# Local/global attention with an MLP: casts of w_out on VectorE, half of batch 1's planes on GpSimd and VectorE, output groups in one piece, global values 64 columns wide

## The chip, the cores and the metric

The kernel runs on one core of one Trainium2 chip. Its time is the device time of one execution in microseconds (us). Of the kernel before, three runs are known, 959.68, 959.82 and 957.89 us, with a median of 959.68. Beside them one execution was taken with the hardware profiler.

## The reference

There are 8 batches of 8 heads with a head size of 64. Each has 512 local tokens and 32 global ones; q, k and v are given apart for both. After the attention every token goes through an MLP with w_in (512 x 2048) and w_out (2048 x 512). Cut to what matters:

```python
def sm(s):
    s = s - np.max(s, axis=-1, keepdims=True)
    e = np.exp(s)
    return e / (np.sum(e, axis=-1, keepdims=True) + 1e-09)

out_g = sm(scale * q_g @ k_all.T) @ v_all           # a global token sees all 544 keys
s_ll = np.where(abs(i - j) <= 32, scale * q_l @ k_l.T, -1e9)
s_lg = scale * q_l @ k_g.T                          # a local one sees the 32 global keys
out_l = sm(concat([s_lg, s_ll])) @ v_all            # and a band of 65 local ones
x = concat([out_g, out_l]).reshape(8 * 544, 512)
h = x @ w_in
return (h * np.cos(h)) @ w_out
```

## The kernel before, in words

**Two planes for each number.** Every matrix that the tensor engine (PE) multiplies is split into a high and a low plane of 16-bit floats, hi = cast(z) and lo = cast(z - hi). A product takes three matmuls: hi by hi, hi by lo and lo by hi. The engines beside PE are ScalarE (ACT), VectorE (DVE) and GpSimd (POOL); all DMAs are issued by SyncE (SP).

**The weights.** They arrive as 64-bit floats. `decode` (L227 to L232) makes 32-bit floats from such a piece: ACT reads the high words (L227), DVE shifts the low words (L228) and joins them (L232). `split_w` (L238) then casts the high plane on ACT (L239) and subtracts it on POOL in two halves (`pool_tt`, L213). Before that, each piece's maximum is taken by DVE (L246), for which pieces 8 to 15 of w_out are loaded once more (`raw_wm`, L388). `w_out_piece` (L397 on) decodes the sixteen pieces of 128 rows of w_out, two in each of the slots 1 to 8, that is, while the first chunks of the MLP already run.

**The attention.** It goes by pairs of heads, four pairs in a batch. `load_qk` brings q and k of a pair (L441, three buffers), `load_v` v of a batch. `v_a` finds the maximum of v: for batches 0 and 1 by four ACT instructions (L476) and a small reduction, from batch 2 on by one DVE reduction (L481); QMA sets which batches take which. `sc_a` multiplies q and k (L527) for four tiles of 128 queries, each against a window of 192 or 224 keys; the exponentials (L425) are on ACT. `sc_d` (L567 on) scales them by the reciprocal sum and writes both planes. It has several forms, chosen by a table. Form 1, which all of batch 1 takes, is two ACT instructions for the high planes (L592) and two DVE ones for the low planes (L593). Form 3 multiplies on POOL (L578), casts on ACT (L584) and subtracts on POOL (L586). Then the planes are transposed by DMA, and `av_a` (L624 on) multiplies them by v (L645). The global queries have their own steps: `g_f` (L728 on) multiplies the transposed weights `ptg` by v into `gacc` (L737), `g_g` scales the result into `xg` (L750).

**The MLP.** Tokens go through in chunks of 256, sixteen of local tokens and one of the globals, with eight slots to a chunk; a slot is 256 of the 2048 hidden columns. In a slot, `m1_a` is 24 matmuls into `ph` (L801, three PSUM buffers). ACT, DVE, ACT, POOL, DVE, ACT and POOL then make h cos(h) in planes `gh` and `gl` (L823 to L846). Three slots later `m2_a` (L849 on) is twelve matmuls of 512 columns into `po_0` and `po_1` (L860 hi by w_out's hi, L861 hi by its lo, L862 lo by its hi). `po` has two buffers, so chunk 1's `m2_a` can't begin before chunk 0's is finished and read out.

**The order of the work.** Each step has a slot and a priority, given by calls `at(slot, priority, function, ...)` (L941 on). A scheduler then puts every instruction in a fixed order on its engine, by these priorities and by when it reckons the inputs to be there. Batch 0's attention lies ahead of slot 0, batch 1's in the slots of chunks 0 and 1, beside the pieces of w_out; later batches run spread out, one ahead of their chunks.

Of the kernel before, what the change touches and what calls it, by code (L numbers as in the profile page):

```python
# [10 lines left out]
F32 = mybir.dt.float32  # L11
# [4 lines left out]
ALU = mybir.AluOpType  # L16
# [3 lines left out]
P = 128  # L20
# [3 lines left out]
SG = 32  # L24
D = 64
# [3 lines left out]
NJ = DF // P  # L29
# [29 lines left out]
PL0 = 0  # L59
PL1 = 1  # L60
VE = [1, 4, 4]
# [6 lines left out]
TPV = [1, 0, 1, 0]  # L68
WLV = 0
DI = 3  # L70
QMA = 2
KQB = 3
# [46 lines left out]
def body(tc, qf, v, wi, wo, mask, out):  # L119
# [5 lines left out]
    with ExitStack() as ctx:  # L125
# [111 lines left out]

        def split_w(h, l, z, on_vector=False):  # L238
            nc.scalar.copy(h, z)  # L239
            if on_vector:  # L240
                nc.vector.tensor_tensor(l, z, h, op=ALU.subtract)
            else:
                pool_tt(l, z, h, ALU.subtract)
# [153 lines left out]
        def w_out_piece(j):  # L397
# [6 lines left out]
            decode(z, raw, wsc, low_after="wsc")  # L404
            split_w(wo_h[:, j], wo_l[:, j], z, j % 4 < WLV)

# [108 lines left out]
        def sc_a(b, p, i):  # L515
# [7 lines left out]
            for j, c in ((i, slice(0, w0)), (i + 1, slice(w0, w0 + w1_))):  # L523
                z, w = WIN[j]
                for h in range(2):
                    r = slice(D * h, D * h + D)
                    nc.tensor.matmul(  # L527
                        pt[h][:, c], q[r, QZ[j] : QZ[j] + P], k[r, z : z + w], start=True, stop=True,
                        skip_group_check=True,
                    )  # L530
# [36 lines left out]
        def sc_d(b, p, i):  # L567
# [3 lines left out]
            w = WIN[i][1]  # L571
            pl = PLS[p][i] if b == 0 else (PL0, PL1, PL)[min(b, 2)]
            if pl in (3, 4):
                if pl == 3:
                    r = rr[:, 2 * i : 2 * i + 2]
# [7 lines left out]
                lo = planes[i][:, :, 1, OFF[i] : OFF[i] + w]  # L583
                nc.scalar.copy(hi, t)  # L584
                for h in range(2):
# [38 lines left out]
        def av_a(b, p):  # L624
# [5 lines left out]
            )  # L630
            for k, (tl, segs) in enumerate(plan):
                for ip, (vt, pl) in enumerate(((vh, 0), (vh, 1), (vl, 0))):
# [95 lines left out]
        def g_f(b, g):  # L728
            ptg = st.pop(("ptg", b, g))
            acc = ps.tile([P, 2, SG], F32, tag="att", name=f"gacc_{b}_{g}")  # L730
            for a in range(2):
                vh, vl = st["v", b, 2 * g + a]
                for tl in range(NT):
                    for ip, (vt, pl) in enumerate(((vh, 0), (vh, 1), (vl, 0))):
                        for h in range(2):
                            hh = 2 * a + h
                            mm = nc.tensor.matmul(  # L737
                                acc[64 * h : 64 * h + 64, a],
                                vt[:, tl, 64 * h : 64 * h + 64],
                                ptg[:, pl * NT + tl, 32 * hh : 32 * hh + 32],  # L740
                                start=(a == 0 and tl == 0 and ip == 0),
                                stop=(a == 1 and tl == NT - 1 and ip == 2),
                                skip_group_check=True,
# [5 lines left out]
        def g_g(b, g):  # L749
            nc.vector.tensor_scalar(  # L750
                xg[:, 2 * g : 2 * g + 2, b * SG : (b + 1) * SG], st.pop(("gacc", b, g)),
                pvs[:, b : b + 1], None, op0=ALU.mult,
            )

# [94 lines left out]
        def m2_a(c, j):  # L849
            gh, gl = st.pop(("g2", c, j))  # L850
            if j == 0:
                st["po", c] = [
                    ps.tile([P, DM], F32, tag="po", name=f"po_{c}_{k}", bufs=2) for k in range(CT // P)
                ]
            po = st["po", c]
            for k in range(CT // P):
                for a in range(2):
                    q = slice(a * CT + k * P, a * CT + (k + 1) * P)
                    f = 2 * j + a
                    nc.tensor.matmul(po[k], gh[:, q], wo_h[:, f], start=(f == 0), stop=False)  # L860
                    nc.tensor.matmul(po[k], gh[:, q], wo_l[:, f], start=False, stop=False)  # L861
                    nc.tensor.matmul(po[k], gl[:, q], wo_h[:, f], start=False, stop=(f == NJ - 1))  # L862

# [221 lines left out]
```

## Time and profile before

| what | before |
|---|---|
| median of three runs | 959.68 us (957.89 to 959.82) |
| the profiled execution | 959.23 us |
| its span (first to last instruction) | 957.5 us |
| mean granted clock of PE | 0.965 |
| PE busy | 909.4 us (95%) |
| ACT busy | 668.4 us (70%) |
| DVE busy | 569.3 us (59%) |
| POOL busy | 399.7 us (42%) |

A busy share is that of the whole span; it hides that the first fifth of the span is not like the rest. The page's second part shows this in 40 equal slices: PE is at nine tenths or more from the seventh slice on, and mostly lower before. Which engine sets the pace is read for each stage from a view that cuts the span at given times. A row of the timeline has a start, a length, the engine, the line and the operation, with what ended the idle time ahead of it in brackets. Matmuls overlap, and their ends are modelled, so the pace of PE is the difference of two starts.

### The profile page before, as it was taken

How to read it: one execution, taken by the hardware profiler on the slowest of the kernel's cores; microseconds unless marked ns; L12 is line 12 of the kernel's file. 1: busy time of each engine (PE TensorE's matmuls, PEld its weight loads, DVE VectorE, ACT ScalarE, POOL GpSimd, SP SyncE). 2: the span in 40 equal slices, each digit the busy share in tenths (PEclk: the TensorE clock that was granted, in tenths of full speed). 3: DMA queues.
4: the chain of work that ended last, by engine and by line, in shares of the span. 5: the costliest groups of instructions: out<-in, count | busy, mean ns of one | idle time of the engine just before them, and what ended most of it. 6: DMA issues, size and time to landing. Idle time of an engine off the chain costs nothing.

```text
span 957.5 us, 20487 instructions
## 1 busy us (share of the span) xinstructions
PE 909.4 (95%) x7963; PEld 604.0 (63%) x7963; DVE 569.3 (59%) x1544; ACT 668.4 (70%) x1435; POOL 399.7 (42%) x412
## 2 busy tenths in 40 slices
PE   6657989999999999999999999999999999999995
PEld 4446656656666666666666666666666666766663
DVE  5987978746565656566655656564746554423231
ACT  7886899957787677766777778777777775443341
POOL 5856654443334243434343333324343434444441
PEclk8667989999999999999999999999999999999998
DMA  9936167745232533545262725342443333000000
GB/s 371 386 121 198 34 163 162 152 111 125 49 108 43 157 63 71 108 122 111 56 122 50 183 46 129 46 146 46 119 61 71 81 68 58 23 1 23 1 24 22
DMA packets 155178, 96.44 MB, mean 101 GB/s; under 512 B 141000, under 2 KB 141128, under 8 KB 153288
## 3 DMA queue, kind: packets, MB, share of 16 engines
q1 hardware_dynamic: 155080, 95.13, 39.6%
q8 instruction: 62, 1.02, 0.4%
q14 instruction: 36, 0.29, 0.1%
HBM read 51.59 MB, written 8.91 MB: 63 GB/s over the span
## 4 chain that ended last, share of the span: by engine, by line
PE 51%; ACT 15%; DVE 11%; issue 9%; POOL 8%; DMA 5%; SPq 0%; ACTq 0%; POOLq 0%; DVEq 0%
PE ph L801 21%; PE po L861 8%; PE po L862 8%; PE po L860 8%; ACT t L425 4%; DMA vr<-v 3%; POOL w L839 3%; PE ps L527 3%; POOL gl L846 2%; ACT planes L592 2%; PE acc L645 2%; DVE gf L841 2%; ACT gh L845 2%; ACT L425 2%; POOL wi_l L213 2%
## 5 line engine op out<-in xcount | busy, mean ns | idle before, releaser
L801 PE MATMUL ph<-xh,wi_h 128*128 128x256 f16 x1024 | 280.7, 274 | 0.9 <-DVE gf L841 0.5
L801 PE MATMUL ph<-xl,wi_h 128*128 128x256 f16 x1024 | 279.8, 273 | 0.0
L801 PE MATMUL ph<-xh,wi_l 128*128 128x256 f16 x1024 | 279.8, 273 | 0.0
L846 POOL TENSOR_TENSOR gl<-gf,gh 128x512 f16<-128x512 f32 x136 | 163.4, 1202 | 237.1 <-ACT gh L845 237.0
L839 POOL TENSOR_TENSOR w<-w 128x512 f32<-128x512 f32 x136 | 143.6, 1056 | 259.1 <-ACT w L425 241.2
L801 PEld LDWEIGHTS <-wi_h 128*128 128x128 f16 x2176 | 205.9, 98 | 55.4 <-issue 18.8
L861 PE MATMUL po<-wo_hl,gh 128*128 128x512 f16 x544 | 206.7, 380 | 0.6 <-POOL wo_hl L213 0.6
L860 PE MATMUL po<-wo_hl,gh 128*128 128x512 f16 x544 | 204.7, 380 | 1.7 <-ACT wo_hl L239 1.7
L862 PE MATMUL po<-wo_hl,gl 128*128 128x512 f16 x544 | 206.3, 380 | 0.0
L845 ACT CAST gh<-gf 128x512 f16<-128x512 f32 x136 | 83.4, 615 | 112.8 <-DVE gf L841 112.7
L824 DVE SCALAR_TENSOR_TENSOR u<-u,cm,ph 128x512 f32<-128x512 f32 x136 | 101.1, 744 | 101.0 <-ACT u L823 101.0
L841 DVE SCALAR_TENSOR_TENSOR gf<-w,ph 128x512 f32<-128x512 f32 x136 | 93.1, 684 | 110.6 <-POOL w L839 110.1
L425 ACT ACTIVATE w<-u,ca 128x512 f32<-128x512 f32 x136 | 98.1, 722 | 84.4 <-DVE u L824 83.5
L425 ACT ACTIVATE t<-t,mn 128x192 f32<-128x192 f32 (+1 forms) x256 | 117.3, 463 | 18.5 <-DVE mn L545 18.1
L801 PEld LDWEIGHTS <-wi_l 128*128 128x128 f16 x1088 | 106.7, 98 | 13.4 <-issue 0.5
L823 ACT ACTIVATE u<-ph,cm 128x512 f32<-128x512 f32 x136 | 92.3, 679 | 25.2 <-PE ph L801 25.2
L593 DVE SCALAR_TENSOR_TENSOR planes<-t,sm,planes 128x192 f16<-128x192 f32 (+1 forms) x232 | 97.8, 481 | 12.0 <-ACT planes L592 11.2
L545 DVE CUSTOM_DVE_ANT_0 t<-ps,msk 128x192 f32<-128x192 f32 (+1 forms) x256 | 83.2, 367 | 18.0 <-PE ps L527 14.8
L862 PEld LDWEIGHTS <-gl 128*128 128x128 f16 x544 | 53.3, 98 | 63.1 <-issue 0.9
L592 ACT ACTIVATE planes<-t,sm 128x192 f16<-128x192 f32 (+1 forms) x232 | 86.3, 458 | 0.0
L861 PEld LDWEIGHTS <-gh 128*128 128x128 f16 x544 | 53.3, 98 | 51.5 <-issue 2.5
L860 PEld LDWEIGHTS <-gh 128*128 128x128 f16 x544 | 52.8, 98 | 51.4 <-issue 2.6
(149 smaller groups left out, 1098.5 us busy)
## 6 DMA issues: line engine op xcount, KB each, us to landing
qkr<-qf SPq DMA_DIRECT2D x31, 608.0 KB, 5.0
vr<-v SPq DMA_DIRECT2D x8, 1280.0 KB, 6.5
out<-o SPq DMA_DIRECT2D x34, 256.0 KB, 2.0
raw_wi<-wi SPq DMA_DIRECT2D x6, 1024.0 KB, 12.2
wo_hl<-wo SPq DMA_DIRECT2D x8, 512.0 KB, 12.7
raw_wm<-wo SPq DMA_DIRECT2D x8, 512.0 KB, 5.7
raw_wo<-wo SPq DMA_DIRECT2D x8, 512.0 KB, 4.4
raw_wi<-wi SPq DMA_DIRECT2D x4, 512.0 KB, 12.3
```

The costliest lines, as they stand in the source:

```text
L425: ins = nc.scalar.activation(*a, **k).ins
L592: a = nc.scalar.activation(hi, t[:, h], AF.Identity, scale=r)
L593: d = nc.vector.scalar_tensor_tensor(lo, t[:, h], r, hi, op0=ALU.mult, op1=ALU.subtract)
L801: nc.tensor.matmul(ph[:, a], w[:, kc, f], x[:, kc, q], start=first and ip == 0, stop=last and ip == 2, skip_group_check=True,)
L824: nc.vector.scalar_tensor_tensor(u, u, m, ph, op0=ALU.subtract, op1=ALU.subtract)
L839: nc.gpsimd.tensor_tensor(w, w, w, op=ALU.mult)
L841: nc.vector.scalar_tensor_tensor(gf, w, 0.5, st.pop(("ph", c, j)).rearrange("p a b -> p (a b)"), op0=ALU.subtract, op1=ALU.mult,)
L845: nc.scalar.copy(gh, gf)
L846: nc.gpsimd.tensor_tensor(gl, gf, gh, op=ALU.subtract)
L860: nc.tensor.matmul(po[k], gh[:, q], wo_h[:, f], start=(f == 0), stop=False)
L861: nc.tensor.matmul(po[k], gh[:, q], wo_l[:, f], start=False, stop=False)
L862: nc.tensor.matmul(po[k], gl[:, q], wo_h[:, f], start=False, stop=(f == NJ - 1))
```

## The change

It has five parts.

- All sixteen high planes of w_out are cast by DVE (L239 before, L243 after) in place of ACT.
- Batch 1's tiles 0 and 2 of each pair take a new form 5 of `sc_d`: POOL multiplies, DVE casts both halves at once, POOL subtracts. Tiles 1 and 3 stay in form 1.
- In chunks 0 and 1 the six products of a slot for one `po` buffer are taken in another order (`MR`, `terms`), which begins with a product that needs the later of the slot's two pieces of w_out.
- `g_f` multiplies v's high plane by both planes of the weights in one matmul of 64 columns; `gacc` gets a further dimension of two, which `g_g` adds with a second DVE instruction.
- Batch 1's maximum of v goes to DVE (QMA), and its scores and its values by v are done in reversed order (SR, AR).

```diff
-PL1 = 1
+PL1 = [5, 1, 5, 1]
+MR = 2
+SR = (1,)
+AR = (1,)
+WH = "DDDDDDDDDDDDDDDD"
-QMA = 2
+QMA = 1
...
-        def split_w(h, l, z, on_vector=False):
-            nc.scalar.copy(h, z)
+        def split_w(h, l, z, on_vector=False, cast="A"):
+            {"A": nc.scalar.copy, "D": nc.vector.tensor_copy, "G": nc.gpsimd.tensor_copy}[cast](h, z)
...
-            split_w(wo_h[:, j], wo_l[:, j], z, j % 4 < WLV)
+            split_w(wo_h[:, j], wo_l[:, j], z, j % 4 < WLV, WH[j])
...
-                for h in range(2):
+                for h in (1, 0) if b in SR else (0, 1):
...
-            pl = PLS[p][i] if b == 0 else (PL0, PL1, PL)[min(b, 2)]
-            if pl in (3, 4):
-                if pl == 3:
+            pl = PLS[p][i] if b == 0 else PL1[i] if b == 1 else PL
+            if pl in (3, 4, 5):
+                if pl in (3, 5):
...
-                nc.scalar.copy(hi, t)
+                (nc.vector.tensor_copy if pl == 5 else nc.scalar.copy)(hi, t)
...
-            for k, (tl, segs) in enumerate(plan):
+            for k, (tl, segs) in enumerate(plan[::-1] if b in AR else plan):
...
-            acc = ps.tile([P, 2, SG], F32, tag="att", name=f"gacc_{b}_{g}")
+            acc = ps.tile([P, 2, 2, SG], F32, tag="att", name=f"gacc_{b}_{g}")
...
-                    for ip, (vt, pl) in enumerate(((vh, 0), (vh, 1), (vl, 0))):
+                    for ip, (vt, n) in enumerate(((vh, 2), (vl, 1))):
...
-                                acc[64 * h : 64 * h + 64, a],
+                                acc[64 * h : 64 * h + 64, a, :n],
-                                ptg[:, pl * NT + tl, 32 * hh : 32 * hh + 32],
+                                ptg[:, tl : tl + NT * (n - 1) + 1 : NT, 32 * hh : 32 * hh + 32],
...
+            nc.vector.tensor_scalar(x, acc[:, :, 1], pv, None, op0=ALU.mult)
+            nc.vector.scalar_tensor_tensor(x, acc[:, :, 0], pv, x, op0=ALU.mult, op1=ALU.add)
...
+            terms = [(a, g, w) for a in range(2) for g, w in ((gh, wo_h), (gh, wo_l), (gl, wo_h))]
+            if c < MR:
+                terms = [terms[i] for i in (4, 5, 2, 1, 3, 0)]
             for k in range(CT // P):
...
+                for i, (a, g, w) in enumerate(terms):
+                    nc.tensor.matmul(
+                        po[k], g[:, a * CT + k * P : a * CT + (k + 1) * P], w[:, 2 * j + a],
+                        start=(j == 0 and i == 0), stop=(j == NS - 1 and i == 5),
+                    )
```

The scheduler orders anew, so the change moves more than it edits. Three places are shown. Line numbers of the new kernel are four to six higher than those of the same lines before, and the number at the end of a name differs between the kernels.

The first is the end of w_out's decoding. On ACT before, from the last piece's first step to its cast (`z_wo_1854`; `wo_hl` holds both planes of w_out); `planes_76` to `planes_82` are the four tiles of a pair, `t` the exponentials:

```order
L227 ACTIVATE z_wo_1854<-raw_wo_1852,wsc 128x512
L592 ACTIVATE planes_76<-t_3_0_2200,sm_3_2376 128x192 x2
L592 ACTIVATE planes_78<-t_3_1_2204,sm_3_2376 128x224 x2
L592 ACTIVATE planes_80<-t_3_2_2214,sm_3_2376 128x224 x2
L592 ACTIVATE planes_82<-t_3_3_2218,sm_3_2376 128x192 x2
L511 ACTIVATE vh_2_3050<-vr_1717,vs_1863 128x640
L823 ACTIVATE u_5_2420<-ph_5_2395,cm_1249 128x512
L845 CAST gh_2_2107<-gf_2_2110 128x512
L714 ACTIVATE planes_g<-gt_1_2079,gsm_1_2385 128x544
L665 ACTIVATE xh_1993<-acc_2_2436,xs 128x512
L239 CAST wo_hl<-z_wo_1854 128x512
```

On ACT after, at the same place; the last piece is `z_wo_1813` here, its cast on DVE:

```order
L429 ACT_TABLE_LOAD
L429 ACTIVATE w_4_2243<-u_4_2242,ca_1201 128x512
L849 CAST gh_1_1983<-gf_1_1986 128x512
L596 ACTIVATE planes_78<-t_3_1_2165,sm_3_2320 128x224 x2
L231 ACTIVATE z_wo_1813<-raw_wo_1811,wsc 128x512
L596 ACTIVATE planes_82<-t_3_3_2179,sm_3_2320 128x192 x2
L718 ACTIVATE planes_g<-gt_1_2040,gsm_1_2329 128x544
L849 CAST gh_2_2068<-gf_2_2071 128x512
L515 ACTIVATE vh_1_2602<-vr_1674,vs_1822 128x640
L515 ACTIVATE vh_2_2977<-vr_1674,vs_1822 128x640
```

The cast of w_out is gone from ACT, and so are the writes of tiles 0 and 2 (`planes_76`, `planes_80`). On DVE before, from the low words of the last piece on:

```order
L228 TENSOR_SCALAR raw_wo_1852<-raw_wo_1852 128x512
L564 TENSOR_SCALAR sm_3_2376<-sm_3_2376 128x8
L565 RECIPROCAL sm_3_2376<-sm_3_2376 128x8
L750 TENSOR_SCALAR xg<-gacc_0_2314,pvs 128x2x32
L709 TENSOR_SCALAR gsm_1_2385<-gsm_1_2385 128x1
L710 RECIPROCAL gsm_1_2385<-gsm_1_2385 128x1
L512 SCALAR_TENSOR_TENSOR vl_1_2657<-vr_1717,vs_1863,vh_1_2656 128x640
L232 SCALAR_TENSOR_TENSOR z_wo_1854<-z_wo_1854,raw_wo_1852 128x512
L593 SCALAR_TENSOR_TENSOR planes_76<-t_3_0_2200,sm_3_2376,planes_76 128x192
L841 SCALAR_TENSOR_TENSOR gf_4_2391<-w_4_2280,ph_4_2254 128x512
L593 SCALAR_TENSOR_TENSOR planes_76<-t_3_0_2200,sm_3_2376,planes_76 128x192
```

On DVE after:

```order
L243 CAST wo_hl<-z_wo_1804 128x512
L569 RECIPROCAL sm_3_2320<-sm_3_2320 128x8
L714 RECIPROCAL gsm_1_2329<-gsm_1_2329 128x1
L232 TENSOR_SCALAR raw_wo_1811<-raw_wo_1811 128x512
L549 ISA t_0_0_2269,mn_0_0_2270<-ps_0_0_1_2259,msk 128x192
L549 ISA mn_0_0_2270 128x1
L549 ISA t_0_1_2273,mn_0_1_2274<-ps_0_0_1_2259,msk 128x224
L549 ISA mn_0_1_2274 128x1
L597 SCALAR_TENSOR_TENSOR planes_78<-t_3_1_2165,sm_3_2320,planes_78 128x224 x2
L236 SCALAR_TENSOR_TENSOR z_wo_1813<-z_wo_1813,raw_wo_1811 128x512
L597 SCALAR_TENSOR_TENSOR planes_82<-t_3_3_2179,sm_3_2320,planes_82 128x192 x2
L243 CAST wo_hl<-z_wo_1813 128x512
```

The cast of a piece (L243) stands behind its join (L236), and the last one ahead of the cast of tile 0 (L588, `planes_76`, which is the next row but one).

The second place is SP's queue about the loads for the maxima of w_out; `qkr_1` is q and k of pair 1. Before:

```order
L388 DMA raw_wm_1008<-wo 128x512
L388 DMA raw_wm_1011<-wo 128x512
L388 DMA raw_wm_1014<-wo 128x512
L441 DMA qkr_1_1413<-qf 128x1216
L388 DMA raw_wm_1017<-wo 128x512
L441 DMA qkr_2_1576<-qf 128x1216
```

After:

```order
L392 DMA raw_wm_1008<-wo 128x512
L392 DMA raw_wm_1011<-wo 128x512
L392 DMA raw_wm_1014<-wo 128x512
L392 DMA raw_wm_1017<-wo 128x512
L445 DMA qkr_1_1369<-qf 128x1216
L406 DMA raw_wo_1515<-wo 128x512
L445 DMA qkr_2_1533<-qf 128x1216
```

The load of the last maximum (`raw_wm_1017`) stands ahead of the load of pair 1, and one load of a piece (`raw_wo_1515`) ahead of that of pair 2.

The third place is PE at the end of chunk 0's output. Before, the last matmuls into `po_0` and `po_1`, which take w_out's last piece; `acc_3` is a pair's values, and the last matmul of chunk 1's `ph_7` stands 35 rows above the first row:

```order
L861 LDWEIGHTS gh_7_1786
L861 MATMUL po_0_1382<-wo_hl,gh_7_1786 128x512
L862 LDWEIGHTS gl_7_1787
L862 MATMUL po_0_1382<-wo_hl,gl_7_1787 128x512
L861 LDWEIGHTS gh_7_1786
L861 MATMUL po_1_1383<-wo_hl,gh_7_1786 128x512
L862 LDWEIGHTS gl_7_1787
L862 MATMUL po_1_1383<-wo_hl,gl_7_1787 128x512
```

After, the end of the last group of twelve (it begins 18 rows above) and what follows:

```order
L865 LDWEIGHTS gh_7_1745
L865 MATMUL po_1_1338<-wo_hl,gh_7_1745 128x512
L865 LDWEIGHTS gh_7_1745
L865 MATMUL po_1_1338<-wo_hl,gh_7_1745 128x512
L865 LDWEIGHTS gh_7_1745
L865 MATMUL po_1_1338<-wo_hl,gh_7_1745 128x512
L805 LDWEIGHTS wi_h
L805 MATMUL ph_7_2522<-xh_1038,wi_h 128x256
```

The eight products of the slot that stood apart ahead of these four are now in one piece with them, and chunk 1's `ph_7` (24 matmuls) comes behind the group.

More of the change, by code (lines that the diff above doesn't have):

```diff
@@ L737, in g_f @@
                             mm = nc.tensor.matmul(
-                                acc[64 * h : 64 * h + 64, a],
+                                acc[64 * h : 64 * h + 64, a, :n],
                                 vt[:, tl, 64 * h : 64 * h + 64],
-                                ptg[:, pl * NT + tl, 32 * hh : 32 * hh + 32],
+                                ptg[:, tl : tl + NT * (n - 1) + 1 : NT, 32 * hh : 32 * hh + 32],
                                 start=(a == 0 and tl == 0 and ip == 0),
-                                stop=(a == 1 and tl == NT - 1 and ip == 2),
+                                stop=(a == 1 and tl == NT - 1 and ip == 1),
                                 skip_group_check=True,
@@ L749, in g_g @@
         def g_g(b, g):
[L750 to L753, printed above, removed]
+            acc, pv = st.pop(("gacc", b, g)), pvs[:, b : b + 1]
+            x = xg[:, 2 * g : 2 * g + 2, b * SG : (b + 1) * SG]
+            nc.vector.tensor_scalar(x, acc[:, :, 1], pv, None, op0=ALU.mult)
+            nc.vector.scalar_tensor_tensor(x, acc[:, :, 0], pv, x, op0=ALU.mult, op1=ALU.add)
         mp = None
@@ L855, in m2_a @@
             po = st["po", c]
+            terms = [(a, g, w) for a in range(2) for g, w in ((gh, wo_h), (gh, wo_l), (gl, wo_h))]
+            if c < MR:
+                terms = [terms[i] for i in (4, 5, 2, 1, 3, 0)]
             for k in range(CT // P):
[L857 to L862, printed above, removed]
+                for i, (a, g, w) in enumerate(terms):
[3 more added lines that the diff above has]
+                    )
         def m2_b(c, k):
```

## The prediction

> **What bounds the kernel now.** I read the busy share in 40 slices first: the tensor engine (PE) is at 9 from the seventh slice (144 us) on and mostly below that ahead of it. So the view of stretches came next, for the two stages that end where PE becomes full, and for one of the full part. The columns are the stretch, its length, then busy time and instructions of PE, PE's weight loads, VectorE (DVE), ScalarE (ACT) and GpSimd (POOL), the granted clock, the DMA share and the rate:
>
> ```profile
> 92.00:128.00 36.00, 34.45 (x289) 22.36 (x288) 34.19 (x77) 31.28 (x61) 24.23 (x26) 0.96 0.20 65
> 128.00:186.00 58.00, 53.36 (x477) 33.78 (x475) 48.39 (x151) 57.79 (x134) 26.09 (x30) 0.94 0.75 164
> 306.00:408.40 102.40, 102.29 (x939) 67.91 (x938) 62.73 (x175) 75.08 (x167) 38.05 (x34) 1.00 0.45 96
> ```
>
> In the full part PE is busy 102.29 of 102.40 us: there only fewer or shorter PE instructions shorten the run, and DVE and ACT have over a quarter free. Between 128 and 186 us ACT works 57.79 of 58.00: this stage is ACT's. Between 92 and 128 DVE is the fullest but for PE (34.19 of 36.00). PE is idle for 1.55 + 4.64 = 6.2 us in both, which bounds what they can give, beside a clock of 0.94 to 0.96 there.
>
> Then the waits of the second stage and the chain that ended last, to see what ACT holds up (waits: total, times, longest; chain: start, length, engine, line):
>
> ```profile
> POOL wo_hl L213 <- ACT wo_hl L239: 15.1, 7, 4.7
> ```
>
> ```profile
> 177.65 2.60 ACT planes L592 x7
> ...
> 183.65 0.52 ACT wo_hl L239
> ...
> 186.15 0.38 PE po L861
> 186.53 0.22 PE po L862
> ```
>
> The last piece of w_out is decoded by DVE, waits for ACT behind seven plane writes, is cast by ACT, subtracted by POOL, and at 186.15 PE takes it. From there on PE is full: call 186.15 the gate. It opens the chunk's PSUM buffers for chunk 1. A move of the gate is a gain only less the PE work that is left behind it.
>
> **Global values, 64 columns at once.** PE's timeline of one group, and of the local values, which already have 64 columns (start, length; lengths overlap, so differences of starts count):
>
> ```profile
> 367.18 0.22 PE L737 MATMUL gacc<-ptg,vh 128*64 128x32 f16 x4
> 367.24 0.19 PE L737 MATMUL gacc<-ptg,vl 128*64 128x32 f16 x2
> ...
> 379.85 0.23 PE L645 MATMUL acc<-pt,vh 128*64 128x64 f16 x4
> 379.91 0.20 PE L645 MATMUL acc<-pt,vl 128*64 128x64 f16 x2
> ```
>
> A round is two vl matmuls and four vh; the four took 0.06 us (367.18 to 367.24). Four matmuls of 64 columns took 0.06 too (379.85 to 379.91), so 64 columns cost what 32 do; two of them instead of four save 0.03 a round and 0.30 us a group, which has ten rounds (two pairs of heads by five tiles of keys). The groups that lie behind the gate are counted by the next row, of the lines from 186 us on:
>
> ```profile
> L750 DVE TENSOR_SCALAR xg<-gacc,pvs 128x64 f32<-128x64 f32 x13 | 3.6, 278 | 0.0
> ```
>
> Thirteen groups in the part where PE is full: 13 x 0.30 = **-3.9 us**. The other bound is that 64 columns cost twice 32, which saves 0; I take the first, since its row is the same shape on the same engine. The read-out becomes two DVE instructions, 0.28 us more for each group. It is hidden under PE in the full part (DVE 62.73 of 102.40); without that cover it would be 16 x 0.28 = 4.5 us.
>
> **The start.** The last maximum of w_out waits for its load, which SyncE issues behind one of q and k, and the maximum of batch 1's v (L481) now lies on DVE near 47 us, where ACT did it. DVE's timeline, SyncE's, and the group of L481:
>
> ```profile
> 49.73 0.39 DVE L545 CUSTOM_DVE_ANT_0 t<-ps,msk 128x224 f32<-128x224 f32 x1 [1.76 <-POOL planes L586]
> 54.10 0.36 DVE L545 CUSTOM_DVE_ANT_0 t<-ps,msk 128x192 f32<-128x192 f32 x1 [0.44 <-POOL planes L586]
> 83.83 0.69 DVE L246 TENSOR_REDUCE wos<-raw_wm 128x1 f32<-128x512 f32 x1 [1.51 <-DMA raw_wm<-wo]
> 87.99 0.69 DVE L246 TENSOR_REDUCE wos<-raw_wm 128x1 f32<-128x512 f32 x1 [3.47 <-DMA raw_wm<-wo]
> ```
>
> ```profile
> 80.25 0.33 SPq L388 DMA_DIRECT2D raw_wm<-wo  x1
> 82.63 0.33 SPq L441 DMA_DIRECT2D qkr<-qf  x1
> 83.06 0.37 SPq L388 DMA_DIRECT2D raw_wm<-wo  x1
> ```
>
> ```profile
> L481 DVE TENSOR_REDUCE vm<-vr 128x1 f32<-128x2560 f32 x6 | 16.9, 2820 | 14.8 <-DMA vr<-v 14.8
> ```
>
> The load without one of q and k ahead of it was used 3.6 us after its issue (80.25 to 83.83), the one behind it 4.9 us (83.06 to 87.99). In the new order it takes the place of 82.63 and is used near 86.2: 1.8 us earlier. The qkr load goes back by one issue, 0.4 us, and its two other buffers hide that; were they not full ahead of need, 0.4 us comes back. L481 costs 2.82 us, of which 1.76 + 0.44 = 2.2 fills idle time: +0.6. Scales and first piece: **1.2 us earlier** (0 if another chain holds the start, 1.8 if L481 is hidden whole).
>
> **From ACT to DVE and POOL.** The rows: the cast and lo planes that go, then the nearest of those that come.
>
> ```profile
> L239 ACT CAST wo_hl<-z_wo 128x512 f16<-128x512 f32 x16 | 9.7, 614 | 2.6 <-DVE z_wo L232 2.6
> ```
>
> ```profile
> L593 DVE SCALAR_TENSOR_TENSOR planes<-t,sm,planes 128x192 f16<-128x192 f32 (+1 forms) x32 | 12.9, 449 | 0.6 <-ACT planes L592 0.6
> L592 ACT ACTIVATE planes<-t,sm 128x192 f16<-128x192 f32 (+1 forms) x32 | 11.9, 457 | 0.0
> ```
>
> ```profile
> L720 DVE CAST planes_g<-gt 128x544 f16<-128x544 f32 x12 | 5.3, 444 | 0.4
> L578 POOL TENSOR_TENSOR t<-t,sm 128x224 f32<-128x224 f32 x6 | 3.2, 562 | 0.0
> L578 POOL TENSOR_TENSOR t<-t,sm 128x192 f32<-128x192 f32 x6 | 2.9, 508 | 8.6 <-DVE sm L565 8.6
> L586 POOL TENSOR_TENSOR planes<-t,planes 128x192 f16<-128x192 f32 x12 | 8.6, 741 | 5.6 <-ACT planes L584 5.6
> L586 POOL TENSOR_TENSOR planes<-t,planes 128x224 f16<-128x224 f32 x12 | 7.5, 645 | 0.9 <-ACT planes L584 0.9
> ```
>
> Over both stages (94 us) ACT works 31.28 + 57.79 = 89.1 us. Sixteen casts (16 x 0.614 = 9.8) and half of the 32 plane writes (16 x 0.457 = 7.3) go: 72.0 of 94, no longer the bound. POOL works 24.23 + 26.09 = 50.3 and gets 8 x 0.562 + 8 x 0.508 + 8 x 0.741 + 8 x 0.645 = 19.6: 69.9, or 1.39 times as much. DVE works 34.19 + 48.39 = 82.6, loses 16 x 0.449 = 7.2, and gets 16 casts of 512 columns (0.444 x 512/544 = 0.42, so 6.7), eight of both halves of a tile (on average 416 columns, 0.34, so 2.7) and 0.8 of read-outs: 85.6. DVE is now the fullest, and what it does beside a busier POOL decides. What that costs already:
>
> ```profile
> L232 DVE SCALAR_TENSOR_TENSOR z_wo<-z_wo,raw_wo 128x512 uint32<-128x512 uint32 x8 | 7.4, 920 | 0.0
> L228 DVE TENSOR_SCALAR raw_wo<-raw_wo 128x512 uint32<-128x512 uint32 x8 | 4.7, 581 | 3.7 <-DMA raw_wo<-wo 3.7
> ```
>
> ```profile
> 135.69 0.42 DVE L228 TENSOR_SCALAR raw_wo<-raw_wo 128x512 uint32<-128x512 uint32 x1
> 144.34 1.14 DVE L228 TENSOR_SCALAR raw_wo<-raw_wo 128x512 uint32<-128x512 uint32 x1
> 178.15 0.68 DVE L232 SCALAR_TENSOR_TENSOR z_wo<-z_wo,raw_wo 128x512 uint32<-128x512 uint32 x1
> ```
>
> ```profile
> 144.16 1.04 POOL L839 TENSOR_TENSOR w<-w 128x512 f32<-128x512 f32 x1 [2.04 <-ACT w L425]
> ```
>
> The same L228 took 0.42 alone and 1.14 beside a POOL instruction, from 144.16 to 145.20. On average L232 is 0.24 and L228 0.16 above the undisturbed 0.68 and 0.42: 0.40 on 1.10 us, or 0.36 us for each us of such work. The 24 casts are 6.7 + 2.7 = 9.4 us of it, and POOL is busy 1.39 times as much: 9.4 x 0.36 x 1.39 = 4.7 us, 0.20 a cast (bounds: 0 when they fall between POOL's instructions, 24 x 0.72 = 17.3 when each waits as the one at 144.34). I choose the mean since it is over 16 instructions among the same neighbours. DVE 85.6 + 4.7 = 90.3 of 94: the stage ends **3.7 us earlier**. The multiply, cast and subtract of eight tiles run through two engines more than before; in each pair of heads tiles 0 and 2 go the new way and 1 and 3 the old, so half of the planes are ready as before while the others come, and I cost the longer way at 0; without that cover it would be the cast's wait behind other work of DVE, up to the 0.72 us above.
>
> The Trainium skill, "SBUF — State Buffer", section "Who interferes with whom", speaks against the move: DVE and GpSimd share one port pair, a cast or tensor_scalar in a two-port mode holds it for the whole instruction, and the other "fully blocks". The row at 144.34 agrees (0.72 us over 0.42); by the rule alone the sum would be the slow rival's.
>
> **One piece, and what is given back.** In chunks 0 and 1 PE takes the twelve matmuls of a slot in one piece, when both pieces of w_out are complete. Before, four of the last twelve were left at the gate, and the first matmuls of ph_7 of chunk 1 stood ahead. Now all twelve stand behind, and ph_7's 24 too. Prices: the chain counts 0.22 us for one of po (186.53); for m1 two rows of PE's timeline, 0.11 apart:
>
> ```profile
> 189.74 0.27 PE L801 MATMUL ph<-xh,wi_h 128*128 128x256 f16 x1
> 189.85 0.27 PE L801 MATMUL ph<-xl,wi_h 128*128 128x256 f16 x1
> ```
>
> 8 x 0.22 = 1.7 and 24 x 0.11 = 2.6: **4.3 us** more PE work behind the gate (0 if that work would have found idle PE time later, but there is none in the full part). Of the 1.2 + 3.7 = 4.9 us by which the gate comes earlier, 0.6 stays. The reversed orders of batch 1's scores and values change no instruction; cost 0, hidden in PE's idle 4.64 us, else some 0.1 us each.
>
> **Sum.** -3.9 - 0.6 = -4.5 us. The profiled run took 959.23 us, 957.5 of it the span, so 954.7 by that run. The median of the runs, 959.68, lies 0.45 above it: 955.2. A measurement here tells 0.2% from no change: 1.9 us, so under 957.8 is faster and over 961.6 slower.
>
> **Rivals.** *The relief comes whole.* No extra wait on DVE: 94 - 85.6 = 8.4 and 1.2 earlier, less 4.3, is 5.3; with 3.9 it is -9.2, 950.5 by the median. PE's idle 6.2 us and 1.8 of the start bound it at -3.9 - 8.0, 947.8. For it: POOL has a quarter free and casts are short. Against: L228's and L232's means.
>
> *DVE and POOL stop each other* (slower). Each new cast is stopped for 0.72 as at 144.34: 85.6 + 17.3 = 102.9 of 94, the gate 8.9 - 1.2 = 7.7 us late, 4.3 given back, 3.9 saved: +8.1, 967.8. It decides from a gate 1.5 us late on (1.5 + 4.3 - 3.9 = 1.9), which is 24 casts at 0.46 us. For it: DVE becomes the fullest engine, POOL is at 74%. Against: the means of 0.16 and 0.24, where the same engines met.
>
> *64 columns cost twice 32.* Then only the 0.6 is left: 959.1, no change. For it: the columns are as many as before. Against: the row at 379.85.
>
> **How the numbers follow.** Forecast 0.50 (952 to 957.5), whole relief 0.22, equal 0.13, slower 0.15. Faster is the first two, 0.72. The range goes from 947, just under the first rival's bound, to 962, where the second begins: it leaves out that rival and some hundredths of the first.
>
> **What would show it.** Right: vh matmuls of 64 columns in pairs of 0.03; from 92 us to the gate ACT under 85% and DVE over 90%; the last piece at PE near 181, with twelve matmuls of po in a row. Casts of w_out by DVE near 0.42 to 0.6 on average. Wrong: casts over 0.88 us, a gate behind 187.6, POOL's subtractions waiting for DVE as long as now for ACT (15.1), or PE with idle time behind the gate.

## The result, and the profile after

The changed kernel takes 964.70 us (median of five runs, 962.72 to 964.78) against 959.68 us of before (957.89 to 960.30): a ratio of 1.0051, with a 95% interval of 1.0039 to 1.0062. It is 5.0 us slower, where 4.5 us faster was forecast and 962 was the range's upper end. The profiled execution took 962.72 us, the fastest of the five, with a span of 960.9 us, 3.4 us longer than before's. One execution of run e7 further down took 1847.55 us, where its other five took 963.10 to 966.38; it is slow and counts in no number here.

Two instructions on VectorE cut the span where it changes its nature. Each slot of a chunk has one `gf` (L841 before, L845 after). First the rows of before's timeline, the last `gf` of chunk 2 and the first of the last chunk:

```profile
257.35 0.67 DVE L841 SCALAR_TENSOR_TENSOR gf<-w,ph 128x512 f32<-128x512 f32 x1
...
904.56 0.69 DVE L841 SCALAR_TENSOR_TENSOR gf<-w,ph 128x512 f32<-128x512 f32 x1 [1.97 <-POOL w L839]
```

The same two of after:

```profile
266.94 0.68 DVE L845 SCALAR_TENSOR_TENSOR gf<-w,ph 128x512 f32<-128x512 f32 x1
...
908.02 0.69 DVE L845 SCALAR_TENSOR_TENSOR gf<-w,ph 128x512 f32<-128x512 f32 x1 [1.96 <-POOL w L843]
```

The part up to the first row, called the head from here on, became 9.6 us longer (266.94 - 257.35). The part between the two, the dense part, became 6.1 us shorter (647.21 to 641.08). The tail is the same. So the change is a gain and a larger loss, and the loss lies in the head. These parts are those of one execution, 2.0 us under the median of its kernel, and hold to about that much.

The stretches of after, in the columns of the prediction:

```profile
92.00:128.00 36.00, 32.29 (x262) 22.91 (x260) 35.36 (x82) 25.21 (x50) 21.25 (x23) 0.95 0.29 81
128.00:186.00 58.00, 45.83 (x410) 29.83 (x409) 54.91 (x132) 48.40 (x108) 48.71 (x61) 0.94 0.60 139
186.00:204.00 18.00, 16.20 (x85) 8.36 (x86) 10.15 (x23) 8.74 (x24) 11.23 (x12) 0.91 0.48 107
```

ACT is relieved (48.40 of 58 where it was 57.79), VectorE is full (54.91), GpSimd went from 26.09 to 48.71. PE, which should have gained, fell from 53.36 to 45.83 us of work in the second stretch. What PE waits for, first in before and then in after, both from 92 to 204 us (total, times, longest; the three longest of before, and of after the three longest and the one for w_out):

```profile
PE acc L645 <- DMA pt<-planes: 2.6, 2, 2.4
PE po L860 <- ACT wo_hl L239: 1.7, 2, 1.1
PE po L861 <- POOL wo_hl L213: 0.6, 1, 0.6
```

```profile
PE ph L805 <- DVE gf L845: 9.4, 4, 3.5
PE ps L531 <- DVE xg L757: 3.0, 1, 3.0
PE gacc L741 <- DMA ptg<-planes_g: 2.7, 1, 2.7
...
PE po L865 <- POOL wo_hl L217: 0.7, 2, 0.4
```

PE's waits for w_out's pieces, 2.3 us before, are down to 0.7 us. New ones of 15 us stand in their place, and the largest are waits for a PSUM buffer that VectorE must read first: the next `m1` wants one of three `ph` buffers, and the `gf` that frees it stands in VectorE's queue. VectorE's timeline ahead of one such wait, GpSimd's row of the `w` that this `gf` needs, and PE's row that the `gf` ends:

```profile
126.00 0.41 DVE L243 CAST wo_hl<-z_wo 128x512 f16<-128x512 f32 x1
126.63 1.02 DVE L597 SCALAR_TENSOR_TENSOR planes<-t,sm,planes 128x224 f16<-128x224 f32 x1 [0.22 <-ACT planes L596]
127.58 0.72 DVE L243 CAST wo_hl<-z_wo 128x512 f16<-128x512 f32 x1
128.22 2.12 DVE L597 SCALAR_TENSOR_TENSOR planes<-t,sm,planes 128x224 f16<-128x224 f32 x3
130.26 0.68 DVE L845 SCALAR_TENSOR_TENSOR gf<-w,ph 128x512 f32<-128x512 f32 x1
```

```profile
126.36 1.04 POOL L843 TENSOR_TENSOR w<-w 128x512 f32<-128x512 f32 x1 [0.59 <-ACT w L429]
```

```profile
130.99 0.37 PE L805 MATMUL ph<-xh,wi_h 128*128 128x256 f16 x1 [3.54 <-DVE gf L845]
```

Two casts of w_out and four low planes lie in front of the `gf`, and the low planes themselves are slow: 1.02 us for one whose like takes 0.45 alone. The `w` was done at 127.40, and VectorE had no idle time from 126.63 until the `gf` began at 130.26: for 2.9 us it stood in the queue. At the two next waits of this kind, which PE ends at 149.48 and 166.32, the `gf` came 6.6 and 5.2 us after its `w`; before, in the same stage (the `gf` from 101 to 180 us), it was 5.6 us once and under 3 us else. The same at the end of the head: the two read-out instructions of the globals (L756, L757) are held up by VectorE's queue, two plane casts (L588) among it. The matmuls into `gacc` were over at 181.20, the second read-out begins at 187.32, and PE's scores need the buffer that it frees.

```profile
185.79 0.82 DVE L588 CAST planes<-t 128x384 f16<-128x384 f32 x1
186.54 0.27 DVE L756 TENSOR_SCALAR xg<-gacc,pvs 128x64 f32<-128x64 f32 x1
186.73 0.66 DVE L588 CAST planes<-t 128x448 f16<-128x448 f32 x1
187.32 0.27 DVE L757 SCALAR_TENSOR_TENSOR xg<-gacc,pvs,xg 128x64 f32<-128x64 f32 x1
```

```profile
187.73 1.22 PE L531 MATMUL ps<-qkr 64*128 64x224 f32 x6 [3.03 <-DVE xg L757]
188.89 0.61 PE L865 MATMUL po<-wo_hl,gh 128*128 128x512 f16 x1
```

The gate, the last group of chunk 0, so begins at 188.89 instead of 186.15, with all twelve matmuls still to do. GpSimd had finished the last piece of w_out at 187.15 (186.10 before): 1.0 us of the delay is the piece itself, the rest the scores ahead of the group.

The groups of VectorE's instructions between 92 and 186 us of after, which the prediction had priced by L593, L239 and L720 of before:

```profile
L597 DVE SCALAR_TENSOR_TENSOR planes<-t,sm,planes 128x224 f16<-128x224 f32 (+1 forms) x16 | 12.6, 829 | 0.4 <-ACT planes L596 0.4
...
L243 DVE CAST wo_hl<-z_wo 128x512 f16<-128x512 f32 x16 | 10.7, 672 | 0.0
...
L588 DVE CAST planes<-t 128x384 f16<-128x384 f32 (+1 forms) x7 | 5.2, 741 | 0.0
```

A cast of w_out took 0.672 us (0.42 alone), a plane cast 0.741, and a low plane of the tiles that stayed as they were 0.829, where the 32 of before had 0.449.

The global values cost PE what was forecast. PE's timeline of one group after:

```profile
374.90 0.20 PE L741 MATMUL gacc<-ptg,vh 128*64 128x64 f16 x2
374.93 0.19 PE L741 MATMUL gacc<-ptg,vl 128*64 128x32 f16 x2
374.96 0.20 PE L741 MATMUL gacc<-ptg,vh 128*64 128x64 f16 x2
```

Two matmuls of 64 columns take 0.03 us, a round 0.06 instead of 0.09. From a group's first matmul to the next work of PE it is 1.06 us in before's timeline and 0.74 in after's: 0.32 us a group, 4.2 us for thirteen.

### The profile page after: what moved, and what is told of

Read it like the earlier page. It is cut to its first block, busy times and chain, and to the rows that moved or that the text cites. A ratio compares the mean times of both kernels' runs of the same rounds, so it can differ in the third digit from the quotient of the medians.

```text
span 960.9 us, 19860 instructions
## 1 busy us (share of the span) xinstructions
PE 902.3 (94%) x7643; PEld 600.1 (62%) x7643; DVE 590.2 (61%) x1568; ACT 650.0 (68%) x1395; POOL 424.1 (44%) x444
## 5 line engine op out<-in xcount | busy, mean ns | idle before, releaser
L865 PE MATMUL po<-wo_hl,gh 128*128 128x512 f16 x1088 | 321.2, 380 | 0.8 <-POOL wo_hl L217 0.7
L865 PE MATMUL po<-wo_hl,gl 128*128 128x512 f16 x544 | 201.3, 380 | 0.0
L845 DVE SCALAR_TENSOR_TENSOR gf<-w,ph 128x512 f32<-128x512 f32 x136 | 93.0, 684 | 113.2 <-POOL w L843 113.0
L805 PEld LDWEIGHTS <-wi_l 128*128 128x128 f16 x1088 | 107.2, 99 | 17.5 <-issue 4.4
L597 DVE SCALAR_TENSOR_TENSOR planes<-t,sm,planes 128x224 f16<-128x224 f32 (+1 forms) x216 | 97.4, 511 | 11.9 <-ACT planes L596 11.1
L531 PE MATMUL ps<-qkr 64*128 64x192 f32 (+1 forms) x496 | 76.5, 384 | 9.8 <-DMA qkr<-qf 5.6
L596 ACT ACTIVATE planes<-t,sm 128x224 f16<-128x224 f32 (+1 forms) x216 | 80.6, 455 | 5.3 <-DMA pt<-planes 2.6
## 6 DMA issues: line engine op xcount, KB each, us to landing
raw_wi<-wi SPq DMA_DIRECT2D x4, 512.0 KB, 12.6
```

The costliest lines, as they stand in the source:

```text
L531: nc.tensor.matmul(pt[h][:, c], q[r, QZ[j] : QZ[j] + P], k[r, z : z + w], start=True, stop=True, skip_group_check=True,)
L597: d = nc.vector.scalar_tensor_tensor(lo, t[:, h], r, hi, op0=ALU.mult, op1=ALU.subtract)
L805: nc.tensor.matmul(ph[:, a], w[:, kc, f], x[:, kc, q], start=first and ip == 0, stop=last and ip == 2, skip_group_check=True,)
L845: nc.vector.scalar_tensor_tensor(gf, w, 0.5, st.pop(("ph", c, j)).rearrange("p a b -> p (a b)"), op0=ALU.subtract, op1=ALU.mult,)
L865: nc.tensor.matmul(po[k], g[:, a * CT + k * P : a * CT + (k + 1) * P], w[:, 2 * j + a], start=(j == 0 and i == 0), stop=(j == NS - 1 and i ...
```

## The experiments

Theory A, at the start: VectorE and GpSimd stop each other, and the moved work so costs the head more than ACT's relief brings. Theory B, its rival: the twelve matmuls in one piece hold PE up. Theory C, the new order of the instructions, and theory D, which gives the order's loss to the head in e1 and to the dense part in e5, came when e1 and e5 had been read. The table gives all runs; the ratio is to the kernel before on the same chip, the head and the dense part are those of the profiled execution, against before's 257.35 and 647.21 us. Differences in time between runs are differences of these medians.

| run | median us | ratio (95%) | head | dense |
|---|---|---|---|---|
| changed kernel | 964.70 | 1.0051 (1.0039 to 1.0062) | +9.6 | -6.1 |
| e1 globals alone | 962.60 | 1.0031 (1.0020 to 1.0042) | +10.7 | -5.5 |
| e2 planes back | 958.90 | 0.9994 (0.9984 to 1.0004) | +6.8 | -6.5 |
| e3 casts back | 959.84 | 1.0003 (0.9994 to 1.0012) | +8.1 | -6.2 |
| e4 pieces apart | 966.28 | 1.0065 (1.0053 to 1.0077) | +14.1 | -7.0 |
| e5 globals, old order | 962.81 | 1.0032 (1.0020 to 1.0043) | +1.7 | +0.8 |
| e6 casts, old order | 963.53 | 1.0039 (1.0027 to 1.0051) | +4.4 | +0.5 |
| e7 planes, old order | 965.28 | 1.0058 (1.0045 to 1.0071) | +6.0 | -0.7 |
| e8 all three, old order | 977.21 | 1.0182 (1.0169 to 1.0195) | +15.6 | +0.8 |
| e9 globals, old head | 955.74 | 0.9963 (0.9951 to 0.9976) | +1.9 | -5.5 |
| e10 old work, new order | 967.29 | 1.0084 (1.0070 to 1.0097) | +14.2 | -6.4 |
| e11 GpSimd reads | 967.17 | 1.0080 (1.0065 to 1.0096) | +9.1 | -0.4 |
| e12 GpSimd writes | 964.22 | 1.0054 (1.0040 to 1.0067) | +7.1 | -0.5 |
| e13 no moved work | 958.38 | 0.9981 (0.9972 to 0.9990) | +5.1 | -5.8 |
| e14 one piece, old head | 959.62 | 0.9999 (0.9988 to 1.0010) | +7.4 | -5.5 |

### One part undone, or one part alone: e1 to e4

e1 leaves only the global values of the change:

```diff
-PL1 = [5, 1, 5, 1]
+PL1 = [1, 1, 1, 1]
-MR = 2
-SR = (1,)
-AR = (1,)
-WH = "DDDDDDDDDDDDDDDD"
+MR = 0
+SR = ()
+AR = ()
+WH = "AAAAAAAAAAAAAAAA"
-QMA = 1
+QMA = 2
```

> The changed kernel with every part undone but the 64-column global values. Columns are cheap: 13 groups by 0.30 us, 3.9 us under the kernel before, so near 955.8 us. Rival, 64 columns cost twice 32: no change, 959.7. If the scheduler's new order matters more than either, it lies outside 953 to 960.

e2 has only the first of these edits (PL1) against the changed kernel, e3 only that of WH, e4 only that of MR.

> Batch 1's tiles all in form 1 again (ACT hi, DVE lo), the rest as changed. Theory A, DVE and POOL stop each other: the low planes' 0.41 us of delay each (6.5 us) and the casts of planes (5.9 us) go from DVE's full stage, and POOL loses some 20 us, so the time falls by 4 to 8 us against the changed kernel's 964.7, to 957 to 961; the low planes go back to about 0.45 us. Theory B, the twelve matmuls in one piece hold PE: no more than 1 us, 963.5 to 965.

> w_out's high planes cast by ACT again, the rest as changed. Theory A: DVE loses 10.7 us and ACT gets 9.8 where it has 10 us free, so the time falls by 2 to 6 us, to 959 to 963, less than with the planes back because POOL's added work and the low planes' delay stay. Theory B: 963.5 to 965.

> MR = 0, the products of chunks 0 and 1 in their old order and so free to stand apart, the rest as changed. Theory A: DVE is as full as before, so within 1.5 us of 964.7. Theory B: PE fills its waits again and the time falls by 4 us or more, under 960.7.

e2 is 5.8 us faster than the changed kernel and e3 4.9 us, both as theory A had it. One sign of theory A failed in e2: without form 5 the low planes took 0.70 us, not the 0.45 that it expected. e4 is 1.6 us slower, a hair over the 1.5 that theory A allowed, and PE waits 8.7 us for pieces of w_out in it where the changed kernel has 0.7: theory B falls, for the order at least that the scheduler gives e4. But e1 missed both its forecast and the rival's, and it was the miss that taught most. It moves no work between engines, its dense part is 5.5 us shorter as it should be, and its head is 10.7 us longer, no less than the changed kernel's. The scheduler had ordered the head anew. PE's waits in e1 from 92 to 204 us are of the old kind, and longer (the three longest):

```profile
PE acc L649 <- DMA pt<-planes: 5.5, 3, 2.9
PE po L865 <- ACT wo_hl L243: 4.4, 3, 2.5
PE po L865 <- POOL wo_hl L217: 2.2, 3, 0.9
```

That is theory C: the new order of the head is the cost. Waits are not all of it: PE's granted clock in this window was 0.91 in e1 where it was 0.96 before, and how much of the 10.7 us goes to it was not taken apart.

### The order held: e5 to e8

For these the order in which the kernel before has its instructions was taken from its build, as a table, and put on each engine by dependencies within the engine, which are to make no wait of their own; no run holds that order without any change, so what the table itself costs was not measured. Instructions that are new stand where those that they replace stood, or are free.

```diff
+for i, before in zip(row[1:], row):
+    tc.add_manual_dep(i, before.name, order, reason="held_order")
```

e5 has the global values of 64 columns in that order, e6 only w_out's casts on VectorE, e7 only batch 1's form 5, e8 all three.

> Only the 64-column global values, as in e1, but every engine keeps the order of the kernel before. Theory C, formed after e1: the scheduler's new order of the first 260 us costs what e1 lost. Then the 13 groups by 0.32 us come through: 4.2 us under before, 955 to 956.5. If it is not the order but the read-out in two instructions or the wider buffer, it stays near e1: 961 to 963.

> Only w_out's casts on DVE, each right behind its join, in the order of the kernel before. Theory A, DVE and POOL stop each other: DVE gets 16 casts of 0.67 us, 10.7, on 82.6 of 94 us, about as full as ACT was; 958 to 963, the casts near 0.67 us. Theory C, the order is all: ACT's relief comes through and the time falls, 953 to 957.

> Only batch 1's tiles 0 and 2 in form 5, the other instructions in the order of the kernel before, the new ones of POOL free. Theory A: POOL gets some 24 us, the low planes of tiles 1 and 3 go from 0.45 to over 0.7 us, DVE's excess rises by 6 us or more, the time is no lower than before, 959 to 965. Theory C: 955 to 959.

> The three parts that move work (global values, casts, planes) in the order of the kernel before; the parts that only change orders and the maximum of v stay as before. Theory A: DVE's sum is 82.6 - 7.2 + 9.4 + 10 of delays = 95 of 94 us, so the gate comes no earlier and only the 4.2 us of the global values are left: 955 to 960. Theory C: relief and global values both come through, 950 to 954.

By its time e5 is a miss of theory C (962.81 us, where theory C had 955 to 956.5 and its rival 961 to 963). By its parts half of theory C stands: the head is repaired (+1.7 instead of +10.7), but the dense part is no longer shorter, although each group is by 0.32 us. In the dense part, from 260 to 910 us, PE's waits of e5 and then of before:

```profile
PE gps L712 <- DVE mn L575: 6.1, 4, 1.8
```

```profile
PE gps L682 <- DVE mn L545: 1.4, 3, 0.7
```

In the old order PE comes sooner to the global scores (`gps`), finds no free buffer, and waits 4.7 us more: what 12 groups save there (3.8 us) and a little over. The changed kernel and e1, in the scheduler's own new order, do not have this wait, so that of the 5.5 us by which e1's dense part is shorter some 1.4 are the wait that before has there and 3.8 the groups.

e6, e7 and e8 say that moved work in the old order costs 3.9, 5.6 and 17.5 us. All three lie outside what theory C had for them, a little over what theory A had for e6 and e7, and far over it for e8: together they cost more than the 12.6 us that the three parts cost singly (3.1 + 3.9 + 5.6). Not every sign of theory A came with it: the low planes of e7 took 0.60 us where it had over 0.7. In e8 it is PE's values that wait for transposed planes (12.0 us in 7 waits from 86 to 260 us): the way of form 5 through GpSimd, VectorE and GpSimd is, as I read it, too long for the place where the old order has what needs it.

### The head held alone, and the new order with the old work: e9, e10

e9 is e5 with the table only for steps of slots below 24, the later ones left to the scheduler:

```diff
+steps.append((f.__name__, a, s < 24, list(nc.cur_bb.bb.instructions)[n0:]))
...
+if early and o is not None and o < n:
+    held[e].append((ranks[e][base[e] + o], j, i))
```

e10 holds the changed kernel's own order, but makes the casts and planes as before (PL1 and WH as in e1).

> Global values of 64 columns; the steps of slots below 24 keep the order of the kernel before, all later ones are left to the scheduler. Theory D: the 13 x 0.32 us are real; e1 lost them in the order of the head, e5 in waits that the old order has further on. Then the head is 1.7 us late as in e5 and the rest 5.5 us shorter as in e1: 955 to 957. Rival, the loss goes with the shorter groups wherever they stand: 959 or more.

> The changed kernel in its own order, but the casts of w_out and batch 1's planes are made as before (ACT casts, form 1). Theory A, the moved work is what costs: DVE loses its 10 us of added delays and the time falls to 957 to 961. Theory C, the new order costs it whatever work is done: 963 to 966.

e9 came out as theory D had it in both parts (+1.9 and -5.5) and in the time: 955.74 us, 0.37% (0.24 to 0.49%) under the kernel before and 9.0 us under the changed one. It is the best version here, and it has one part of the five. Its 3.8 us are not the groups alone: the head costs 1.9 us, and the dense part gives back 5.5, of which the groups are 3.8.

e10 missed on the side of theory C: with the old work, the new order is slower still (967.3). In this order the moved work even saves 2.6 us, so what it costs is not a property of the work alone, but of the work in an order. PE's granted clock from 92 to 204 us was 0.88 in e10 (0.94 in the changed kernel), which may be part of its loss; it was not taken apart. Contention is not tied to form 5 either. The low planes of e10, with GpSimd's work as before:

```profile
L622 DVE SCALAR_TENSOR_TENSOR planes<-t,sm,planes 128x224 f16<-128x224 f32 (+1 forms) x26 | 15.6, 652 | 4.0 <-ACT planes L621 4.0
```

0.652 us where before had 0.449. Laid over GpSimd's timeline, from 92 to 190 us, 14 of 30 overlap a GpSimd instruction for a tenth of their length or more and take 0.85 us on average, 16 do not and take 0.42. Before it was 7 of 32 at 0.53 and the others at 0.43; after, 15 of 16 at 0.86. What a low plane costs goes with whether its place falls beside GpSimd's work.

### GpSimd's work by itself: e11, e12

Both are the kernel before in its own order; in their traces VectorE, ScalarE and GpSimd have all instructions of before in the same sequence. e11 adds subtractions behind each piece of w_out, whose result nobody uses; e12 memsets in the same places.

```diff
+idle = mp.tile([P, 256], F32, tag="idle", name=f"idle_{j}", bufs=1)
+for k in range(2):
+    nc.gpsimd.tensor_tensor(idle, zero[:, :256], zero[:, 32:288], op=ALU.subtract)
```

```diff
+for k in range(4):
+    nc.gpsimd.memset(idle, 0.0)
```

> The kernel before in its own order; GpSimd gets, behind each of the 16 pieces of w_out, two subtractions of 256 columns on constants that nobody waits for (some 19 us in the stage, like form 5's). No work of another engine changes. Theory A: DVE's low planes of batch 1 go from 0.45 to over 0.55 us and its delays rise by 5 us or more; time 961 to 967. If GpSimd's queue alone were the matter, DVE's durations stay and only the time rises as in e12.

> As e11, but GpSimd only writes: four memsets of 256 columns behind each piece, and reads no SBUF. Theory A, the two engines meet where GpSimd reads: DVE's durations stay as before and the time is within 1.5 us of before (959.7), under e11's by 2 us or more for the same GpSimd time. Rival, GpSimd's queue is what delays the chain: the same time as e11.

The added groups of GpSimd from 92 to 186 us, and VectorE's low planes there, first e11 and then e12:

```profile
L434 POOL TENSOR_TENSOR idle<-zero 128x256 f32<-128x256 bf16 x30 | 22.3, 744 | 1.2
...
L622 DVE SCALAR_TENSOR_TENSOR planes<-t,sm,planes 128x192 f16<-128x192 f32 (+1 forms) x24 | 11.7, 530 | 1.2 <-ACT planes L621 1.2
```

```profile
L434 POOL MEMSET idle<- 128x256 f32 x60 | 18.9, 315 | 2.6
...
L622 DVE SCALAR_TENSOR_TENSOR planes<-t,sm,planes 128x192 f16<-128x192 f32 (+1 forms) x25 | 11.7, 508 | 1.2 <-ACT planes L621 1.2
```

Work on GpSimd that no one waits for costs 7.7 us in e11 and 4.7 us in e12, against before's 959.50. Theory A had e12 within 1.5 us and e11's low planes over 0.55 us (0.53): there it falls, and GpSimd's queue is the better reading of the larger part. GpSimd was busy 54% of the stage before (50.3 of 94 us), yet its free time was not to be had: `w`, `gl` and w_out's low halves queue behind what is added. In the traces `gl` of the first 13 slots begins on average 0.50 us after its `gh` before, 2.11 us in e11 and 1.78 in e12. The queue is not alone even in e12: the same 250 instructions of VectorE (those that lie between 92 and 200 us before) took 3.1 us longer in e12 and 4.6 in e11. The 3.0 us between e11 and e12 are for both the reading and 3.4 us more of GpSimd's time; the two were not taken apart.

### What the moved work costs where the scheduler orders for it: e13, e14

e13 is the changed kernel with PL1 and WH as in e1. e14 is e9 with MR = 2, whose matmuls of chunks 0 and 1 are free to be placed.

> The changed kernel without the casts and without the planes on DVE and GpSimd (both as before), ordered anew by the scheduler. If the moved work is what lengthens the head, it is faster than e2 (958.9) and e3 (959.8): 953 to 957. If any new order costs the head what e1's did, it stays at 960 to 964.

> e9 with the twelve matmuls of a slot in one piece in chunks 0 and 1; only these matmuls are free to be placed, every other step of the head keeps the old order. If one piece saves PE's waits for w_out's pieces, as e4 against the changed kernel had it (1.6 us): 953 to 955. If it gives back PE work behind the gate, as the prediction had it (4.3 us): 958 to 961.

e13 is 6.3 us faster than the changed kernel, but at 958.38 it lies between its two expectations and settles neither. With e2 (only the casts moved, +0.5 us over e13), e3 (only the planes, +1.5) and the changed kernel (both, +6.3) the four make a square: either move alone costs little, both together more than their sum. By the ratios of the table the steps are 1.2, 2.1 and 6.7 us, each good to some 1.5 us: by either count the single steps add up to less than both moves cost, but by how much less is not settled. PE's waits for `ph` buffers go the same way; from 92 to 204 us, first of e13, then of e2 and e3 (9.4 with both moves):

```profile
PE ph L805 <- DVE gf L845: 4.0, 2, 3.5
```

```profile
PE ph L805 <- DVE gf L845: 4.6, 3, 3.2
```

```profile
PE ph L805 <- DVE gf L845: 3.3, 2, 1.8
```

VectorE is busy 52.27 of 58 us between 128 and 186 with the casts alone, 47.79 with the planes alone, 54.91 with both; GpSimd 29.71, 44.76 and 48.71. My reading is that either engine may be full, but not the two that hand work to each other; the scheduler ordered each of the four anew, so the square does not show it by itself. Nor does the moved work explain the whole head: e13, without it, is still 5.1 us late there. PE's wait for the transposed weights of the globals (`gacc` for `ptg`, 2.7 us in the changed kernel) is in e13 too (3.7 us) and in e2, e3 and e4, but not in before or e1; it goes with the reversed orders or the moved maximum, which these five share.

e14 is 3.9 us slower than e9, so that one piece costs in a held head about what the prediction gave for it, while with the changed kernel's other parts it saves 1.6 us (e4). The way is another than the prediction's: PE is busy 93.61 us from 92 to 204 in e14 and 103.64 in e9, and its waits for planes and `ph` buffers are 13.0 us where e9 has 5.1.

## Why the prediction was wrong, step by step

- **"-3.9 us" for the global values** was right: 0.32 us instead of 0.30 a group, 4.2 us for thirteen, and e9, in which they stand alone in a held head, is 3.8 us faster, if by a balance of head and dense part. The rival "64 columns cost twice 32" is out by the rows at 374.90.
- **The start, "1.2 us earlier"**, was right for the scales and wrong for the first piece: VectorE's timeline has the last scale of w_out (`wsc`) at 93.08 us before and at 90.93 after, 2.15 us earlier, but the first piece was complete at 103.36 instead of 102.94. PE's first `po` came at 108.37 instead of 101.61: the group now needs both pieces (104.62), and PE has other work ahead of it.
- **"DVE 85.6 + 4.7 = 90.3 of 94: the stage ends 3.7 us earlier" is the step that failed.** Its sum was right to the tenth (35.36 + 54.91 = 90.27 us), and that is luck: low planes that were not touched cost 16 x (0.829 - 0.449) = 6.1 us more, for which the step had nothing, the casts cost some 2 us more than it had, and some 7 us of other work that VectorE did between 92 and 186 us before (four mask instructions, two `vl`, two shifts and more) lay outside these 94 us after. And the inference was wrong. At 90.3 of 94 an engine that others wait for in order was full: PE stood 9.4 us for `ph` buffers whose `gf` was in VectorE's queue, 3.0 us for the globals' read-out, and the gate opened 2.7 us late instead of 4.9 us early. The stage's end was set by the order in VectorE's queue, and a sum of busy time was only its lower bound. e13 puts the price of the moved work at 6.3 us of the 9.5 by which the forecast was missed; the rest is not assigned.
- **"I cost the longer way at 0"** for batch 1's planes, and GpSimd with "a quarter free", failed with it: e11 and e12 price some 20 us of work on GpSimd at 4.7 to 7.7 us even if nobody waits for its result. GpSimd had 50.3 us of work in a stage of 94, and no room for 20 more.
- **The slow rival** had the right sign and pair of engines, but not the place. The casts were delayed by 0.25 us (w_out's) and some 0.4 us (planes, 0.741 against 0.34), under its point of 0.46; the low planes that were not touched, the queue on GpSimd and the waits for `ph` buffers, which it did not have, stand beside it in the trace. The row at 144.34 agreed with the section that the prediction cites, "Who interferes with whom" in "SBUF — State Buffer" of the Trainium skill. These runs agree further: a low plane has two inputs in SBUF, and took 0.42 us alone, 0.86 beside GpSimd.
- **"4.3 us more PE work behind the gate"** (4.4 by its own prices) has the right size in a held head (e14 against e9: 3.9 us), but e14 loses by PE's waits, so the size is partly luck.
- **The signs**: ACT fell to 78% of the 94 us and VectorE rose to 96%, the casts of w_out took 0.67 us on average, and the last group was one piece, all near what was to show the forecast right. The gate at 188.89, behind 187.6, was the sign of being wrong: the relief of ACT came, the earlier gate did not.
- **That an order keeps its quality when work changes** was assumed without a word. By e1 and e9, which have the same work and the same dense part (-5.5 us both) and differ in the order of the head, a new order of the scheduler's costs 6.9 us.

What stays open: why the scheduler's new head for e1 is so much worse. Its places are known (PE's waits for planes and for pieces of w_out, and a granted clock of 0.91), but not which of its estimates went wrong. Nor was the 4.2 us between e1 and e13, which the reorderings together bring in the scheduler's own order, split into its parts beyond e4.

## What to carry to other kernels

Here a stage in which one engine was at 100% and two others at 83 and 45% was not relieved by moving its work to these two, which hand work to each other in order. Ask for each moved instruction which buffer or result stands behind it in the new queue, and who waits for that. Where a scheduler orders the program, an edit also draws a new order; hold the old one in the part that was tuned, let the rest go free, and the edit's own worth shows, as e9 did with 3.8 us where the same edit without it (e1) lost 2.7. Test moves together as well as one by one, since here 0.5 and 1.5 us came to 6.3.

## What the runs showed of the hardware that was not expected

- GpSimd's memsets did not slow VectorE's low planes, as far as two instructions tell: in e12 the two of 192 columns that overlap nothing but memsets took 0.415 and 0.418 us, and those beside no work of GpSimd 0.403 to 0.416. Beside GpSimd's reading instructions low planes took up to 1.22 us in the same run. The Trainium skill, "SBUF — State Buffer", section "Who interferes with whom", has it so: an instruction of VectorE with two SBUF inputs contends with a GpSimd instruction that reads SBUF, not with one that only writes it.
- The cost falls on both sides. GpSimd's subtractions of batch 1's planes took 0.786 us between 92 and 186 us of after and its multiplies 0.692, where the same lines averaged 0.693 (741 and 645 ns) and 0.535 (562 and 508 ns) before. In the head of after 13 of the 16 subtractions lie beside VectorE's casts, shifts, joins, `vl` or low planes and took 0.86 us, the other three 0.59.
- PE ran slowly after a wait: the twelve `po` matmuls from 188.89 us on, behind the 3.03 us of idle time at 187.73, took 3.9 us to the next group at 192.84 in PE's timeline, where twelve take 12 x 0.22 = 2.6. The granted clock was 0.50 from 188.3 to 191.6 us, and 0.91 from 186 to 204 (1.00 before). This wait of PE so cost some 1.3 us more than its own length. It was 0.50 behind the waits that end at 130.99 and 149.48 too, but 1.00 from 166.3 to 172.0, behind one of 3.02 us: not every such wait is followed by it.
